# Attention with exact fp16 pairs and a gated MLP on one core: products with v seven tiles behind their scores in place of five, and copy, subtraction and transpose written one tile behind the exponential

## The chip, the cores and the metric

The kernel runs on one core of a Trainium2 chip. The metric is the device time of one execution in microseconds. Before the change three runs took 709.54 us in the median (708.9 to 712.29).

## The reference

Inputs are q, k, v of 4 batches, 8 heads, 768 rows, 64 columns, and the weights of a gated MLP. Attention is masked by a hash: a row's six sign bits of `q @ proj` must equal those of the key's row.

```python
mask = q_bucket[:, :, :, None] == k_bucket[:, :, None, :]
scores = scale * np.matmul(q, k.transpose(0, 1, 3, 2))
scores = np.where(mask, scores, -1000000000.0)
attn = softmax(scores)                      # maximum subtracted, exp, divided by the sum + 1e-9
x = attn @ v                                # then heads side by side: (4, 768, 512)
h = relu(x @ w_in); u, v = halves of h      # 512 and 512 columns
v_n = layer norm of v (no gain)
v_s = w_spatial @ v_n + b_spatial           # mixes the 768 rows
out = (u * v_s) @ w_out
```

## The kernel before

Each of the 32 heads is cut into six tiles of 128 query rows. A global count g = 6 * head + tile runs the main loop; iteration g writes the scores of tile g and the products with v of an older tile, and small pieces of everything else between. Values that need more than fp16 are kept as a pair of fp16 numbers, a rounded one and the rest.

A tile of the heads 0 and 8 to 31 goes through this chain:

- `scores` (L300, L301): four matmuls per tile on TensorE (PE), two per half of the keys, from the buffer `ab` of the head into a PSUM buffer `sp` (two of them). The hash mask is part of the second matmul.
- L302: VectorE (DVE) copies the scores to `ex` (four buffers) and takes the row maximum; L303 and L304: ScalarE (ACT) makes the bias `nb` and the exponential, in place.
- L307: ScalarE rounds `ex` to fp16 in `pp` (four buffers); L308: VectorE, or GpSimd (POOL) for one or two tiles of a head, subtracts to get the rest.
- L310: SyncE (SP) issues a transposing DMA from `pp` to `pt` (six buffers).
- `weighted` (L323 to L325): 18 matmuls with `pt` as weights and the split v (`vp`, two buffers, one per pair of heads) into the PSUM buffer `pv`. After a head's last tile, `normalize` divides by the sums and `transpose_x` brings a pair of heads, by another transposing DMA (`xt`), into the form that the MLP needs.

Heads 1 to 7 (KEYS) go another way without a transpose: their scores are made with keys on the partitions (`scores_k`, `weighted_k`), three tiles apart.

When all eight heads of a batch are done, its MLP is put in a queue of 28 units (`vps`, `ups`, `sps`, `ops`), and 28/48 of a unit is taken per iteration. The units of the last batch run after the last attention tile. `build` makes the buffer `ab` for the head two further on (DMAs from `hl` and `sg`); `load_qk`, `load_v`, `hash_rows`, `split_qk` and `split_v` work ahead by one to three pairs of heads.

The order of the instructions on each engine is not that of the text. Every piece is written with a place number, `at(g, k)` = 1000 * (g + 40) + k, and a scheduler issues per engine what has the lowest number and is ready by its own reckoning. `tc.issue_after(x)` keeps what is written inside it from being issued ahead of x. SP issues all loads and transposes in one queue; each waits in line for the one ahead. `st["tr"]` is the transpose written last.

The lines that set the distance are these:

```python
LAG = 5
...
while wv < N * NT and wv + (LAGK if wv // NT in KEYS else LAG) <= g:
```

Of the kernel before, what the change touches and what calls it, by code (L numbers as in the profile page):

```python
# [36 lines left out]
def lsh_attention_spatial_gating(  # L37
# [14 lines left out]
    NT = S // P  # L52
# [47 lines left out]
    st = {}  # L100
# [46 lines left out]
    def load_qk(p):  # L147
        b, r = divmod(p, NPAIR)
        qk = st["qk", p] = ld.tile([P, 2, S], F32, tag="qk", bufs=QKB, name=f"qk{p}")
        LQ.dma_start(out=qk, in_=kq[b, r])  # L150

    def load_v(p):
        b, r = divmod(p, NPAIR)
        if has_queries(p):
            v32 = st["v32", p] = ld.tile([P, 2 * NT, D], F32, tag="v32", bufs=1, name=f"v32_{p}")
            LQ.dma_start(out=v32, in_=v[b, r])

    def load_vf(p):
        b, r = divmod(p, NPAIR)
        if has_keys(p):  # L160
            LQ.dma_start(out=vf[p % 2][:, :, 0:D], in_=v[b, r])
# [4 lines left out]
    def has_queries(p):  # L166
        return not (2 * p in KEYS and 2 * p + 1 in KEYS)

    def hash_rows(p):
        qk = st["qk", p]  # L170
        hp = ps_m.tile([P, 512], F32, tag=MT, name=f"hp{p}")
        for j in range(4):
            nc.tensor.matmul(
                hp[32 * j:32 * j + 32, :HS], lhsT=pj,
                rhs=qk[:, 1 - j // 2, (j % 2) * HS:(j % 2 + 1) * HS],
                start=True, stop=True, tile_position=(0, 32 * j))
        s0 = wk.tile([P, HS], F16, tag="sg0", name=f"sg0_{p}")
        nc.vector.tensor_scalar(s0, hp[:, :HS], 0.0, hv[:, 0:1], op0=ALU.is_gt, op1=ALU.subtract)
        s1 = wk.tile([P, HS], F16, tag="sg1", bufs=2, name=f"sg1_{p}")
        nc.vector.tensor_scalar(s1, s0, hv[:, 1:2], None, op0=ALU.mult)  # L180
        st["sg", p] = s1

    def split_qk(p):
        qk = st["qk", p]
        hl = wk.tile([P, 4, S], F16, tag="hl", bufs=1, name=f"hl{p}")
        nc.scalar.activation(hl[:, 1:3], qk, AF.Copy, scale=SQ)
        nc.vector.scalar_tensor_tensor(out=hl[:, 0], in0=qk[:, 1], scalar=SQ, in1=hl[:, 2], op0=ALU.mult, op1=ALU.subtract)
        nc.vector.scalar_tensor_tensor(out=hl[:, 3], in0=qk[:, 0], scalar=SQ, in1=hl[:, 1], op0=ALU.mult, op1=ALU.subtract)
        st["hl", p] = hl
# [29 lines left out]
    def split_v(p):  # L219
        if not has_queries(p):  # L220
            return
        v32, t = st["v32", p], vp[p % 2]
        nc.scalar.activation(t[:, :, D:2 * D], v32, AF.Copy, scale=SQ)
        nc.vector.scalar_tensor_tensor(out=t[:, :, 0:D], in0=v32, scalar=SQ, in1=t[:, :, D:2 * D], op0=ALU.mult, op1=ALU.subtract)
# [38 lines left out]
    def scores_k(n, i):  # L263
        t = ab[n % NAB]
        ps = ps_sc.tile([P, 2, 512], F32, tag="sc", name=f"sp{n}_{i}")[:, :, :HS]
        ks = slice(i * P, (i + 1) * P)
        for c in range(2):
            cs = slice(c * HS, (c + 1) * HS)
            nc.tensor.matmul(ps[:, c], lhsT=t[:, 1, ks], rhs=t[:, 0, cs], start=True, stop=False)  # L269
            nc.tensor.matmul(ps[:, c], lhsT=t[:, 2, ks], rhs=t[:, 3, cs], start=False, stop=True)  # L270
        ex = wk.tile([P, S], F32, tag="pt", bufs=PTB, name=f"ex{n}_{i}")
        st["ex", n, i] = nc.scalar.activation(ex.rearrange("p (c q) -> p c q", c=2), ps, AF.Exp, scale=ISQ).ins
        st["pt", n, i] = ex
# [11 lines left out]
    def scores(n, i):  # L285
        if n in KEYS:
            scores_k(n, i)
            return
        t = ab[n % NAB]
        if i == 0:  # L290
            st["nb", n] = wk.tile([P, NT], F32, tag="nb", bufs=3, name=f"nb{n}")
            st["mx", n] = wk.tile([P, NT], F32, tag="mx", bufs=4, name=f"mx{n}")
        mx, nb = st["mx", n][:, i:i + 1], st["nb", n][:, i:i + 1]
        ex = wk.tile([P, 2, HS], F32, tag="ex", bufs=EB, name=f"ex{n}_{i}")
        qs = slice(i * P, (i + 1) * P)
        ps = ps_sc.tile([P, 2, 512], F32, tag="sc", name=f"sp{n}_{i}")[:, :, :HS]
        K = P if n % 2 and n >= NH else P - 1
        for c in range(2):
            cs = slice(c * HS, (c + 1) * HS)
            nc.tensor.matmul(ps[:, c], lhsT=t[:, 0, qs], rhs=t[:, 1, cs], start=True, stop=False)  # L300
            nc.tensor.matmul(ps[:, c], lhsT=t[0:K, 3, qs], rhs=t[0:K, 2, cs], start=False, stop=True)  # L301
        nc.vector.tensor_scalar(ex, ps, -float(2 ** 28), None, op0=ALU.max, op1=ALU.max, accum_out=mx)  # L302
        nc.scalar.activation(nb, mx, AF.Copy, scale=-ISQ)  # L303
        st["ex", n, i] = nc.scalar.activation(ex, ex, AF.Exp, bias=nb, scale=ISQ).ins  # L304
        at(NT * n + i + G_H, 50)
        pp = wk.tile([P, 2, 2, HS], F16, tag="pp", bufs=PB, name=f"pp{n}_{i}")
        nc.scalar.copy(pp[:, 0], ex)  # L307
        (nc.gpsimd if i in (PL_POOL if n >= 2 * NH else PL_POOL1) else nc.vector).tensor_tensor(out=pp[:, 1], in0=ex, in1=pp[:, 0], op=ALU.subtract)  # L308
        pt = st["pt", n, i] = wk.tile([P, 2 * NT, P], F16, tag="pt", bufs=PTB, name=f"pt{n}_{i}")
        st["tr"] = nc.sync.dma_start_transpose(out=pt, in_=pp.rearrange("p g c k -> p (g c k)")).ins  # L310
# [147 lines left out]
    N = B * NH  # L458
    NP = B * NPAIR

    PL_POOL = (2,)
    KEYS = {1, 2, 3, 4, 5, 6, 7}
# [14 lines left out]
    EB = 4  # L477
    PTB = 6
    XTB = 6
    LAG = 5  # L480
    XL_ENG = nc.vector
    G_S = 0
    G_H = 1
# [12 lines left out]
    def at(g, k):  # L496
        tc.cur_priority = int(1000 * (g + 40) + k)
# [16 lines left out]
    rml = [(NT * n + i - NT - LEAD, n, i) for n in sorted(KEYS) for i in range(NT)]  # L514
    for g in range(N * NT + LAG):
        n, i = divmod(g, NT)
        if n < N:
            at(g + G_S, 0)
            scores(n, i)
            r = n // 2  # L520
            at(g + G_P, 300)
            if g == 0:
                hash_rows(1)
                split_qk(1)
                split_v(0)
                load_qk(2)
                load_v(1)
                load_vf(0)
                load_vf(1)
            at(g + G_M, 100)  # L530
            while rml and rml[0][0] <= g:
                row_max(*rml.pop(0)[1:])
            at(g + G_P, 300)
            stack = ExitStack()
            if n not in KEYS:
                stack.enter_context(tc.issue_after(st["tr"]))
            if BQ_S[n + 2 >= NH] is nc.scalar or BQ_H[n + 2 >= NH] is nc.scalar:
                stack.enter_context(tc.issue_after(st["ex", n, i]))
            if i == BI and n + 2 < N:
                build(n + 2)  # L540
            if n % 2 == 0:
                if i == 4 and 0 < r < NP - 1:
                    load_vf(r + 1)
                if i == 5 and r + 1 < NP:
                    split_v(r + 1)
                    mean_v(r + 1)
                if i == 4 and r == 0:
                    mean_v(0)
            else:
                if i == 2 and r + 2 < NP:  # L550
                    hash_rows(r + 2)
                if i == 3 and r + 2 < NP:
                    split_qk(r + 2)
                if i == 5 and r + 3 < NP:
                    load_qk(r + 3)
                if i == 1 and r + 2 < NP:
                    load_v(r + 2)
            stack.close()
        while wv < N * NT and wv + (LAGK if wv // NT in KEYS else LAG) <= g:
            m, j = divmod(wv, NT)  # L560
            wv += 1
            at(g + G_V, 200)
            weighted(m, j)
            if j == NT - 1:
                at(g + G_N, 250)
                normalize(m)
                if m % 2:
                    transpose_x(m // 2)
                    if m % NH == NH - 1:
                        queue += mlp_units(m // NH)  # L570
        at(g + G_W, 500)
        while wdone < W_AT(g):
            wdone += 1
            next(wg, None)
        if queue and n < N:
            credit += 28.0 / DEN
            at(g + G_U, 400)
            while queue and credit >= 1.0:
                queue.pop(0)()
                credit -= 1.0  # L580
# [44 lines left out]
```

## Time and profile before

| | |
|---|---|
| median of three runs | 709.54 us |
| profiled execution | 708.95 us |
| its span, first to last instruction | 707.2 us |
| mean granted TensorE clock | 0.964 |
| instructions | 14858 |
| DMA packets, bytes | 286555, 111.51 MB |

The profile's page gives each engine's busy time and share of the span; the waits say for which instruction's end an engine stood idle, with the total, the number of times and the longest. "A <- B" reads "A waited for B". L numbers are lines of the kernel, tile names are those of the program without their numbers, and SPq is the queue of DMA issues on SP. PEld is TensorE's loading of weights, which runs beside its matmuls.

### The profile page before, as it was taken

How to read it: one execution, taken by the hardware profiler on the slowest of the kernel's cores; microseconds unless marked ns; L12 is line 12 of the kernel's file. 1: busy time of each engine (PE TensorE's matmuls, PEld its weight loads, DVE VectorE, ACT ScalarE, POOL GpSimd, SP SyncE). 2: the span in 40 equal slices, each digit the busy share in tenths (PEclk: the TensorE clock that was granted, in tenths of full speed). 3: DMA queues.
4: the chain of work that ended last, by engine and by line, in shares of the span. 5: the costliest groups of instructions: out<-in, count | busy, mean ns of one | idle time of the engine just before them, and what ended most of it. 6: DMA issues, size and time to landing. Idle time of an engine off the chain costs nothing.

```text
span 707.2 us, 14858 instructions
## 1 busy us (share of the span) xinstructions
PE 618.5 (87%) x5735; PEld 391.0 (55%) x5735; DVE 511.3 (72%) x961; ACT 454.2 (64%) x806; POOL 222.0 (31%) x215
## 2 busy tenths in 40 slices
PE   1668798999796989999796999899888999999997
PEld 0236676778453655565454565565445655655553
DVE  4665698388888897779699897899697987725100
ACT  1444477567686868777588786868677688724121
POOL 5111434454324452152002162033022530322513
PEclk9999798699899999999998999999999999999999
DMA  9557557353698979998989999999989899950011
GB/s 242 143 109 185 125 154 161 89 163 106 134 185 176 184 161 199 217 194 192 206 153 214 165 197 191 201 185 215 214 171 151 158 180 206 156 132 1 0 45 45
DMA packets 286555, 111.51 MB, mean 158 GB/s; under 512 B 270356, under 2 KB 273428, under 8 KB 286484
## 3 DMA queue, kind: packets, MB, share of 16 engines
q1 hardware_dynamic: 284180, 109.67, 77.0%
q10 hardware_dynamic: 2304, 0.89, 0.6%
q8 instruction: 45, 0.74, 0.4%
q14 instruction: 26, 0.21, 0.1%
HBM read 28.33 MB, written 6.29 MB: 49 GB/s over the span
## 4 chain that ended last, share of the span: by engine, by line
PE 48%; DMA 22%; DVE 11%; issue 7%; SPq 4%; ACT 4%; POOL 4%; ACTq 0%; DVEq 0%; POOLq 0%
DMA pt<-pp 14%; PE sps L428 7%; PE ops L443 7%; PE vps L372 6%; PE ups L413 6%; PE pv L282 4%; DMA ab<-hl 4%; PE sp L300 3%; PE sp L301 3%; PE pv L323 3%; SPq L310 2%; PE pv L325 2%; PE pv L324 2%; DVE ex L302 2%; PE sp L269 1%
## 5 line engine op out<-in xcount | busy, mean ns | idle before, releaser
L302 DVE TENSOR_SCALAR_CACHE_REDUCE ex<-sp 128x768 f32<-128x768 f32 x150 | 141.8, 951 | 42.1 <-PE sp L301 39.7
L304 ACT ACTIVATE ex<-ex,nb 128x768 f32<-128x768 f32 x150 | 139.3, 932 | 7.4 <-ACT nb L303 4.5
L323 PE MATMUL pv<-vp,pt 128*128 128x65 f16 x900 | 105.7, 196 | 43.3 <-DMA pt<-pp 42.7
L307 ACT CAST pp<-ex 128x768 f16<-128x768 f32 x150 | 123.7, 826 | 10.5 <-DMA pt<-pp 5.2
L308 DVE TENSOR_TENSOR pp<-ex,pp 128x768 f16<-128x768 f32 x116 | 123.1, 1064 | 9.5 <-ACT pp L307 8.9
L308 POOL TENSOR_TENSOR pp<-ex,pp 128x768 f16<-128x768 f32 x34 | 57.9, 1702 | 218.0 <-ACT pp L307 175.3
L323 PEld LDWEIGHTS <-pt 128*128 128x128 f16 x900 | 85.5, 100 | 70.7 <-DMA pt<-pp 61.8
L300 PE MATMUL sp<-ab 128*128 128x384 f16 x300 | 102.1, 340 | 14.4 <-DMA ab<-hl 9.3
L324 PE MATMUL pv<-vp,pt 128*128 128x64 f16 x900 | 105.4, 196 | 0.0
L325 PE MATMUL pv<-vp,pt 128*128 128x65 f16 x900 | 104.8, 197 | 0.0
L301 PE MATMUL sp<-ab 127*128 127x384 f16 (+1 forms) x300 | 102.2, 341 | 0.6 <-DMA ab<-sg 0.6
L428 PE MATMUL sps<-ws,vn 128*128 128x384 f16 x576 | 100.7, 326 | 0.5 <-DVE sy L432 0.5
L324 PEld LDWEIGHTS <-pt 128*128 128x128 f16 x900 | 85.9, 99 | 10.7 <-issue 1.9
L325 PEld LDWEIGHTS <-pt 128*128 128x128 f16 x900 | 86.0, 99 | 2.3 <-issue 0.6
L428 PEld LDWEIGHTS <-vn 128*128 128x128 f16 x576 | 54.3, 98 | 35.1 <-issue 1.8
L282 PEld LDWEIGHTS pv<-vf,ex 128*128 128x128 f32 x504 | 69.2, 210 | 3.2 <-issue 1.0
L372 PE MATMUL vps<-wi,xt 128*128 128x512 f16 x288 | 67.4, 382 | 3.2 <-DMA xt<-xs 3.2
L413 PE MATMUL ups<-xt,wi 128*128 128x384 f16 x384 | 69.4, 333 | 0.0
L443 PE MATMUL ops<-wo,g 128*128 128x512 f16 x288 | 67.8, 379 | 1.0 <-ACT o L447 0.9
L282 PE MATMUL pv<-vf,ex 128*128 128x65 f32 x504 | 68.0, 289 | 0.0
L303 ACT ACTIVATE nb<-mx 128x1 f32<-128x1 f32 x150 | 29.3, 197 | 57.2 <-DVE ex L302 56.2
L433 POOL TENSOR_TENSOR sy<-sy,u 128x384 f32<-128x384 f32 x32 | 35.9, 1125 | 75.5 <-DVE sy L432 54.5
(91 smaller groups left out, 920.8 us busy)
## 6 DMA issues: line engine op xcount, KB each, us to landing
qk<-kq SPq DMA_DIRECT2D x16, 768.0 KB
ab<-hl SPq DMA_DIRECT2D x34, 192.0 KB
out<-o SPq DMA_DIRECT2D x24, 256.0 KB
v<-v SPq DMA_DIRECT2D x13, 384.0 KB
raw<-w_in SPq DMA_DIRECT2D x16, 256.0 KB
ab<-hl SPq DMA_DIRECT2D x7, 384.0 KB
pt<-pp SPq DMA_TRANSPOSE x150
raw<-w_sp SPq DMA_DIRECT2D x12, 192.0 KB
```

Source lines behind the costliest of these rows:

```text
L282: nc.tensor.matmul(acc[:, qi, :], lhsT=ex[:, qi * P:(qi + 1) * P], rhs=vf[p % 2][:, 2 * i + e, :], start=(i == 0 and qi == 0), stop=(i == ...
L300: nc.tensor.matmul(ps[:, c], lhsT=t[:, 0, qs], rhs=t[:, 1, cs], start=True, stop=False)
L301: nc.tensor.matmul(ps[:, c], lhsT=t[0:K, 3, qs], rhs=t[0:K, 2, cs], start=False, stop=True)
L302: nc.vector.tensor_scalar(ex, ps, -float(2 ** 28), None, op0=ALU.max, op1=ALU.max, accum_out=mx)
L304: st["ex", n, i] = nc.scalar.activation(ex, ex, AF.Exp, bias=nb, scale=ISQ).ins
L307: nc.scalar.copy(pp[:, 0], ex)
L308: (nc.gpsimd if i in (PL_POOL if n >= 2 * NH else PL_POOL1) else nc.vector).tensor_tensor(out=pp[:, 1], in0=ex, in1=pp[:, 0], op=ALU.subtract)
L323: nc.tensor.matmul(acc, lhsT=pt[:, c, :], rhs=vh, start=(i == 0 and c == 0), stop=False)
L324: nc.tensor.matmul(acc[:, 0:D], lhsT=pt[:, c, :], rhs=vl, start=False, stop=False)
L325: nc.tensor.matmul(acc, lhsT=pt[:, NT + c, :], rhs=vh, start=False, stop=(i == NT - 1 and c == NT - 1))
L428: nc.tensor.matmul(ps[:, :HS], lhsT=vn[gv][:, c, d * P:(d + 1) * P], rhs=ws[gw][:, c, hs], start=(k == 0), stop=(k == 3 * NT - 1))
L443: nc.tensor.matmul(ps, lhsT=gt[h][gg][:, c, j * P:(j + 1) * P], rhs=wo[gw][:, c, :], start=(k == 0), stop=(k == 3 * NF - 1))
```

## The change

`LAG` becomes 7, so the products of tile t are written in iteration t + 7. The second half of `scores` (copy, subtraction, transpose) becomes a function `halves`, called one iteration later, after the loads and builds of that iteration; its place number is the same as before, (t + 1, 50), since it was put one tile behind already. What is written under `issue_after(st["tr"])` now refers to the transpose of tile g - 2, and not of tile g. `split_v` and `load_v` are tied to `LAG`: the split for the next pair moves from tile 5 of the even head to tile 1 of the odd one, two tiles later, and the load behind it from tile 1 to tile 2.

```diff
         st["ex", n, i] = nc.scalar.activation(ex, ex, AF.Exp, bias=nb, scale=ISQ).ins
-        at(NT * n + i + G_H, 50)
+        st["e32", n, i] = ex
+
+    def halves(n, i):
+        ex = st.pop(("e32", n, i))
         pp = wk.tile([P, 2, 2, HS], F16, tag="pp", bufs=PB, name=f"pp{n}_{i}")
...
-    LAG = 5
+    LAG = 7
+    SPL = 1
...
-            if n not in KEYS:
+            if n not in KEYS and 'tr' in st:
                 stack.enter_context(tc.issue_after(st["tr"]))
...
                 if i == 5 and r + 1 < NP:
-                    split_v(r + 1)
                     mean_v(r + 1)
...
-                if i == 1 and r + 2 < NP:
+                if i == LAG - NT and r + 1 < NP:
+                    split_v(r + 1)
+                if i == LAG - NT + 1 and r + 2 < NP:
                     load_v(r + 2)
             stack.close()
+        if 0 <= g - SPL < N * NT and (g - SPL) // NT not in KEYS:
+            at(g - SPL + G_H, 50)
+            halves(*divmod(g - SPL, NT))
```

The built order shows what the scheduler makes of it. In names such as `pt22_1_5695` the first numbers are head and tile, the last one a running number. On PE, in the middle of head 22, the first products of tile 22_1 stood behind the scores of tile 23_0:

```order
L300 MATMUL sp23_0_5912<-ab3_85 128x384
L301 LDWEIGHTS ab3_85
L301 MATMUL sp23_0_5912<-ab3_85 128x384
L323 LDWEIGHTS pt22_1_5695
L323 MATMUL pv22_5864<-vp1_95,pt22_1_5695 128x65
```

Now, with new line numbers (L326 is the former L323):

```order
L300 MATMUL sp23_2_5942<-ab3_85 128x384
L301 LDWEIGHTS ab3_85
L301 MATMUL sp23_2_5942<-ab3_85 128x384
L326 LDWEIGHTS pt22_1_5672
L326 MATMUL pv22_5896<-vp1_95,pt22_1_5672 128x65
```

The products moved behind two more score tiles. Over all tiles, 93 of 150 stood five score tiles behind and 22 six; now 75 stand seven and 47 six behind.

On SP, in the same place of the program, the order of loads and transposes was this (`xt10` is the transpose of x, `ab` a head's buffer, `v32` and `qk` loads from memory):

```order
L355 DMA_TRANSPOSE xt10_5846<-xs10_5575 128x12x128
L310 DMA_TRANSPOSE pt22_5_5860<-pp22_5_5857 128x12x128
L310 DMA_TRANSPOSE pt23_0_5923<-pp23_0_5920 128x12x128
L217 DMA ab1_83<-hl12_5500 64x1536
L310 DMA_TRANSPOSE pt23_1_5962<-pp23_1_5959 128x12x128
L156 DMA v32_13_5964<-v 128x768
L310 DMA_TRANSPOSE pt23_2_6020<-pp23_2_6017 128x12x128
L310 DMA_TRANSPOSE pt23_3_6061<-pp23_3_6058 128x12x128
L310 DMA_TRANSPOSE pt23_4_6121<-pp23_4_6118 128x12x128
L310 DMA_TRANSPOSE pt23_5_6185<-pp23_5_6182 128x12x128
L150 DMA qk14_6187<-kq 128x1536
```

and is now:

```order
L313 DMA_TRANSPOSE pt22_5_5851<-pp22_5_5848 128x12x128
L313 DMA_TRANSPOSE pt23_0_5894<-pp23_0_5891 128x12x128
L217 DMA ab1_83<-hl12_5438 64x1536
L358 DMA_TRANSPOSE xt10_5878<-xs10_5609 128x12x128
L313 DMA_TRANSPOSE pt23_1_5964<-pp23_1_5961 128x12x128
L156 DMA v32_13_5959<-v 128x768
L313 DMA_TRANSPOSE pt23_2_6000<-pp23_2_5997 128x12x128
L313 DMA_TRANSPOSE pt23_3_6056<-pp23_3_6053 128x12x128
L150 DMA qk14_6085<-kq 128x1536
```

The transpose of x moved two places back and the load of q and k two places forward; `ab` and `v32` kept theirs.

On PE at the end of attention, the last products (tile 31_5) stood between two pieces of the units `ops2_4` and `ops2_3`. The end of the piece ahead of them:

```order
L443 MATMUL ops2_4_8585<-wo1_107,g2_0_1_8167 128x512
L443 LDWEIGHTS g2_1_1_8168
L443 MATMUL ops2_4_8585<-wo0_106,g2_1_1_8168 128x512
L323 LDWEIGHTS pt31_5_8447
L323 MATMUL pv31_8449<-vp1_95,pt31_5_8447 128x65
```

Now the products of 31_4 stand right ahead of them, and all of `ops2_3` to `ops2_5` with the unit `sps2_3_1` behind them:

```order
L327 MATMUL pv31_8425<-vp1_95,pt31_4_8350 128x64
L328 LDWEIGHTS pt31_4_8350
L328 MATMUL pv31_8425<-vp1_95,pt31_4_8350 128x65
L326 LDWEIGHTS pt31_5_8397
L326 MATMUL pv31_8425<-vp1_95,pt31_5_8397 128x65
```

Eighteen matmuls of `ops` moved from ahead of the last products to behind them, and the unit `sps2_3_1` with them, while `sps2_1_1` and two product tiles came behind the last scores.

## The prediction

> **What bounds the kernel now.** I read the page's first lines, then TensorE's own waits by stage, then one wait followed back by hand, then the load of each engine in the stage where the waits lie.
>
> ```profile
> span 707.2 us, 14858 instructions
> PE 618.5 (87%) x5735; PEld 391.0 (55%) x5735; DVE 511.3 (72%) x961; ACT 454.2 (64%) x806; POOL 222.0 (31%) x215
> ```
>
> TensorE (PE) is idle for 707.2 - 618.5 = 88.7 us and no other engine is near it in the mean. The next view sums each stage: 180 to 632 us is the stage of the 144 query tiles with transposes (heads 8 to 31), after it only the last batch's gating stage is left. Columns: stretch, length, busy time of PE, PEld, DVE, ACT, POOL, granted clock, DMA share, GB/s.
>
> ```profile
> 180.00:632.00 452.00, 407.12 (x4379) 249.85 (x4378) 373.70 (x692) 338.57 (x593) 133.72 (x100) 0.97 0.98 183
> 632.00:707.00 75.00, 70.42 (x384) 37.26 (x382) 13.71 (x34) 19.20 (x39) 22.00 (x22) 1.00 0.09 29
> 0.00:180.00 180.00, 140.98 (x975) 103.89 (x976) 123.87 (x237) 96.44 (x176) 66.29 (x93) 0.92 0.58 147
> ```
>
> The middle stage spends 452 / 144 = 3.14 us a tile, and TensorE idles 452 - 407.1 = 44.9 us of it. The last 75 us are TensorE alone, and the change does not alter them. TensorE's waits in the middle stage, the three that are over 1 us:
>
> ```profile
> PE pv L323 <- DMA pt<-pp: 36.6, 32, 3.2
> PE sp L300 <- DVE ex L302: 3.8, 7, 0.9
> PE vps L372 <- DMA xt<-xs: 3.2, 1, 3.2
> ```
>
> So 36.6 of 44.9 us is one thing: the products wait for the transposed exponentials, 32 times, never over 3.2 us. Is that a chain that is too long for the distance between scores and products, or a chain that cannot go faster? Here is tile 1 of head 22, from the timeline (start, duration, engine, line).
>
> ```profile
> 441.28 0.32 PE L300 MATMUL sp<-ab 128*128 128x384 f16 x1
> 442.49 0.33 PE L300 MATMUL sp<-ab 128*128 128x384 f16 x1
> 443.52 0.95 DVE L302 TENSOR_SCALAR_CACHE_REDUCE ex<-sp 128x768 f32<-128x768 f32 x1
> 445.42 0.86 SPq L150 DMA_DIRECT2D qk<-kq  x1
> 445.94 0.93 ACT L304 ACTIVATE ex<-ex,nb 128x768 f32<-128x768 f32 x1 [0.65 <-ACT nb L303]
> 446.76 2.35 SPq L310 DMA_TRANSPOSE pt<-pp  x1
> 447.24 0.82 ACT L307 CAST pp<-ex 128x768 f16<-128x768 f32 x1
> 448.40 0.95 DVE L308 TENSOR_TENSOR pp<-ex,pp 128x768 f16<-128x768 f32 x1
> 449.17 0.91 SPq L217 DMA_DIRECT2D ab<-hl  x1
> 450.17 7.13 SPq L310 DMA_TRANSPOSE pt<-pp  x3
> 452.70 0.20 PE L323 MATMUL pv<-vp,pt 128*128 128x65 f16 x1
> 453.26 0.32 PE L300 MATMUL sp<-ab 128*128 128x384 f16 x1
> 455.78 0.20 PE L323 MATMUL pv<-vp,pt 128*128 128x65 f16 x1 [1.71 <-DMA pt<-pp]
> ```
>
> The scores start at 441.28. Maximum, exponential, copy and subtraction end at 449.35; most of those 8.1 us is queueing, the four operations themselves take 0.95 + 0.93 + 0.82 + 0.95 = 3.65. The transpose is issued at 450.17, behind a transpose (446.76) and a load (449.17) that themselves stood behind a 768 KB load (445.42). The products start at 455.78, 14.5 us after the scores. Meanwhile TensorE had done the five next score tiles (the last, head 23 tile 0, at 453.26) and had nothing else in its order. Five tiles at 3.14 us are 15.7 us: the chain and the distance are equally long, and any burst (a load, a normalization) makes TensorE wait.
>
> **The change, part by part.** *Nothing is added or removed.* Each tile still issues one exponential, copy, subtraction and transpose.
>
> *Seven tiles in place of five.* In the built order the products of that tile stand behind head 23 tile 2: two score tiles further, 2 x 3.14 = 6.3 us more room. Every one of the 32 waits is at most 3.2 us, so each alone would be covered. Two kinds I leave standing. First the ramp into head 8, where there is no lead yet; then the stretches in which VectorE is full, because there TensorE would only wait one step earlier, at the scores. TensorE's waits on pt at 185 to 192, 215 to 226 and 370 to 391 us, and VectorE's load (third busy column) in the latter two:
>
> ```profile
> PE pv L323 <- DMA pt<-pp: 3.1, 2, 2.0
> PE pv L323 <- DMA pt<-pp: 4.6, 3, 2.5
> PE pv L323 <- DMA pt<-pp: 6.0, 4, 2.8
> ...
> 215.00:220.00 5.00, 2.97 (x29) 1.41 (x27) 4.96 (x12) 1.96 (x5) 1.14 (x1) 1.00 0.56 107
> 220.00:225.00 5.00, 2.19 (x26) 1.25 (x26) 5.00 (x9) 5.00 (x11) 2.53 (x2) 1.00 1.09 267
> 370.00:375.00 5.00, 3.73 (x50) 2.20 (x49) 4.96 (x14) 3.34 (x9) 1.64 (x1) 1.00 1.14 235
> 380.00:385.00 5.00, 4.73 (x60) 3.69 (x61) 5.00 (x10) 4.44 (x8) 0.00 (x0) 0.50 1.15 226
> ```
>
> Term 1: -(36.6 - 3.1 - 4.6 - 6.0) = **-22.9 us**. Its bounds: 0, if the chain is at its own limit; -33.5, if all but the ramp goes.
>
> *What is late next.* With 22 us less, VectorE's 373.7 us fill 87% of the stage in place of 83%, and TensorE meets its two score buffers more often. That row is 3.8 us now (sp <- DVE ex); I take it twice: **+3.8**, bounds 0 and +10.6 (the waits left standing above, a second time).
>
> *Copy, subtraction and transpose one tile behind.* The number that places them is (tile + 1, 50) before and after, so only the written order moves. In the built order 134 of 150 copies stood ahead of the next tile's exponential, now 131; on VectorE some subtractions fall behind one more maximum (0.95 us) and some come one forward. Room 6.3 us covers that: 0, bounds -0.95 and +0.95.
>
> *Loads on SP.* What waits for "the last transpose" now waits for one two tiles older, so SP takes the head builds and the q/k loads one to three places earlier, and the transposes of x two tiles later. Around head 23 the order has ab, xt, v and qk with only three pt transposes between them, where xt stood two tiles ahead and qk four behind v. Landing times from the chain of waits:
>
> ```profile
> 1.19 4.39 DMA qk<-kq
> 391.83 4.13 DMA v<-v
> 495.86 4.76 DMA xt<-xs
> ```
>
> A bunch of three can hold up a transpose by some 4 us at most, within the 6.3; **+2**, bounds 0 and 12 pairs x 1.66 (one transpose issue, row below) = +20.
>
> *Six transposed buffers, seven tiles.* The transpose of tile t must now wait until the products of t - 6 are done, and these stand behind the scores of t + 1, no longer ahead of those of t. On SP, in order, everything behind it waits along. In the tile above, the scores of t + 1 start at 442.49; the products of one tile take 0.6 us (452.70 to 453.26), so the buffer would come free near 443.9 (two times 0.7, scores and products, after 442.49), while the subtraction ended at 449.35: 5.4 us to spare. 0, bounds 0 and the rival below.
>
> *v.* The split of v comes two tiles later and its load one tile behind it; the first products that read it are later by two tiles as well, twelve tiles behind the split in both orders, and the products that read what it overwrites still end one tile ahead of it. 0.
>
> *The end.* In the order of before, 18 matmuls of `ops` separate the last products from the tile ahead of them; now the last five product tiles stand in a row and the fillers behind them.
>
> ```profile
> 613.95 0.32 PE L300 MATMUL sp<-ab 128*128 128x384 f16 x1
> 623.18 4.05 PE L443 MATMUL ops<-wo,g 128*128 128x512 f16 x18
> 627.07 0.19 PE L323 MATMUL pv<-vp,pt 128*128 128x65 f16 x1
> L310 SPq DMA_TRANSPOSE pt<-pp x150: 1307/1657/3611, 28.4 to 621.3; - x150
> ```
>
> Last scores to last products are 13.1 us, with 3.9 us of them `ops`; now two product tiles more stand between them and no `ops`, so TensorE arrives 3.9 - 2 x 0.6 = 2.7 us earlier. The last transpose, issued at 621.3, lands at 626.9 if it takes the 5.6 us of tile 22_1, and TensorE would be there at 624.4: at most +2.5. The queues are emptier here, so **+1**, bounds 0 and +2.5; behind it 54 matmuls of fillers cover the last transpose of x.
>
> *The start.* Head 0 is the only tile row there. The waits on pt of 25 to 180 us:
>
> ```profile
> PE pv L323 <- DMA pt<-pp: 6.1, 4, 2.2
> ```
>
> They may go, or the key heads behind head 0 may come up to two tiles later: 0, bounds -6.1 and +6.3.
>
> Sum: -22.9 + 3.8 + 2 + 1 = -16.1, span 691.1. The profiled execution took 708.95 us for a span of 707.2, so 692.8; the median of the runs is 0.6 above that execution: **693.5 us**.
>
> **The clock.** After such waits the granted clock falls: 0.50 in 380 to 385 above, and less sharply around the others.
>
> ```profile
> 215.00:230.00 15.00, 9.54 (x87) 5.22 (x86) 12.98 (x28) 10.42 (x21) 6.88 (x5) 0.89 0.95 190
> 340.00:352.00 12.00, 7.32 (x92) 4.59 (x93) 7.32 (x13) 6.62 (x12) 0.00 (x0) 0.86 1.07 196
> 370.00:395.00 25.00, 17.83 (x196) 11.42 (x195) 21.16 (x47) 20.55 (x37) 6.79 (x5) 0.80 1.18 215
> ```
>
> The missing clock is 0.11 x 15 + 0.14 x 12 + 0.20 x 25 = 8.3 us. Two of the three stretches are those I leave standing, so I take none of it. [...]
>
> **Rivals.**
> *A, TensorE becomes the only bound.* All 33.5 us go and the 8.3 us of clock with them: -33.5 - 8.3 + 3.8 + 1 = -37 us, **672 us**. For it: no wait is longer than 3.2 us. Against: DMA share 0.98 and VectorE full for stretches.
>
> *B, the chain is at its own limit.* The DMA share of the stage is 0.98 and the transposes fill it; a longer distance only stores tiles, and TensorE waits as long in other places. Term 1 is 0, the new waits are 0 too, and the end's +1 stays: **710 us**. Against: while TensorE waits the DMA share is as low as 0.56 (215 to 220), and VectorE idles 78 us of the stage.
>
> *C, slower: SP held by the sixth buffer.* If a transpose has to wait for the products of t - 6, all later loads and transposes wait with it, and the waits move rather than go. It decides once TensorE reaches the products of t - 6 over 5.4 us later than I reckon, say with two 18-matmul units between them. SP's own waits:
>
> ```profile
> SPq L310 <- PE pv L325: 54.9, 40, 3.2
> ```
>
> That row names TensorE's products already, though by the order this buffer is free long before; if it is real and comes in place of the 36.6, the time is 709.5 + 54.9 - 36.6 = **728 us**. [...]
>
> **How the numbers follow.** Forecast 0.52 (685 to 703), A 0.14, B 0.20, C 0.14. A change under 0.5% (3.5 us) cannot be told from none. Faster: 0.52 + 0.14 + 0.02 of B's edge = 0.68; same: most of B, 0.17; slower: C and a little of B, 0.15. The range leaves out the far part of A and most of C: 680 to 712.
>
> **What would show it.** Right: the row pv <- pt of the stage falls from 36.6 to about 14 us, sp <- DVE ex rises to about 8, the stage shortens by some 16 us with TensorE's busy time unchanged, VectorE's share rises to 0.86. B: pv <- pt is smaller but sp <- DVE ex has taken its place. C: transposes start within 1 us after the products of six tiles before, and SP's queue stands still there. I am wrong if the order costs more than I see: late xt for `vps`, or products that wait at the end.

## The result, and the profile after

The changed kernel takes 690.56 us in the median of four runs (689.38 to 695.97), the one before 709.56 (708.9 to 712.29). The ratio is 0.974, with a 95% interval of 0.9683 to 0.9797. The forecast was 693.5 us, so the total was right. What follows shows that the sum behind it was right only in part: the larger share of the gain comes from the half of the change that the prediction priced at next to nothing (0 for the instructions that move, +2 for the loads that this releases).

The profiled execution took 690.15 us. The head of its page:

```profile
span 688.3 us, 14846 instructions
PE 606.2 (88%) x5735; PEld 385.5 (56%) x5735; DVE 517.4 (75%) x961; ACT 451.0 (66%) x806; POOL 229.0 (33%) x215
```

TensorE is idle for 688.3 - 606.2 = 82.1 us, only 6.6 less than before; the other 12.3 us went out of its busy time, although it runs the same 5735 matmuls. The missing clock (one minus the granted clock, times the length; 0.964 was granted before, 0.972 after) fell by 707.2 x 0.036 - 688.3 x 0.028 = 6.2 us. That it accounts for half of the 12.3 is an estimate, which takes a us of missing clock as one of busy time; for the rest the rows name no cause. A forecast by waits alone cannot have seen any of it.

To see where, both executions are cut at the same four events: the first scores of head 8 (175.9 us before, 164.3 after), the last scores, the last products, the end. Columns as in the prediction: stretch, length, busy PE, PEld, DVE, ACT, POOL, granted clock, DMA share, GB/s. The kernel before:

```profile
0.00:175.90 175.90, 136.88 (x942) 100.31 (x943) 119.90 (x228) 95.29 (x174) 65.39 (x93) 0.92 0.58 147
175.90:613.90 438.00, 393.16 (x4225) 242.49 (x4224) 368.80 (x684) 332.20 (x581) 128.57 (x95) 0.97 0.98 185
613.90:627.70 13.80, 13.80 (x174) 9.09 (x171) 7.40 (x13) 5.93 (x11) 6.05 (x7) 1.00 0.76 117
627.70:707.20 79.50, 74.69 (x405) 39.12 (x401) 15.18 (x38) 20.80 (x42) 22.00 (x22) 1.00 0.11 35
```

and the changed one:

```profile
0.00:164.30 164.30, 127.17 (x944) 94.11 (x945) 118.03 (x215) 92.08 (x166) 64.95 (x90) 0.95 0.61 155
164.30:590.20 425.90, 386.49 (x4171) 240.28 (x4170) 376.55 (x696) 331.88 (x587) 133.99 (x97) 0.98 1.02 191
590.20:601.90 11.70, 11.24 (x192) 8.46 (x188) 6.98 (x13) 5.62 (x10) 5.97 (x6) 1.00 0.95 163
601.90:688.30 86.40, 81.26 (x439) 42.67 (x436) 15.89 (x39) 21.41 (x43) 24.05 (x25) 1.00 0.10 33
```

The differences are -11.6, -12.1, -2.1 and +6.9, together -18.9 us. Two of the four rows were put at zero in the prediction: the first stage, which gives the same as the middle one, and the tail, which got longer. TensorE's busy time in the middle stage falls by 6.7 us and rises by 6.6 in the tail: matmuls of the MLP have moved to the end.

TensorE's waits in the middle stage of the changed kernel (164 to 590 us; total, times, longest); those of before are the three rows in the prediction:

```profile
PE pv L326 <- DMA pt<-pp: 18.3, 19, 2.1
PE sp L300 <- DVE ex L302: 11.3, 14, 2.3
PE vps L375 <- DMA xt<-xs: 5.6, 3, 4.1
PE sps L431 <- DVE sg L178: 2.2, 2, 1.3
PE ups L416 <- DVE sg L178: 1.1, 1, 1.1
```

The waits for the transposes are halved (36.6 to 18.3), and 13.2 us of other waits stand in their place: VectorE at the scores 3.8 to 11.3, the transposed x 3.2 to 5.6, and `sg`, 3.3 us that were not in the list (the signs of a hash, read from a buffer in the pool that the MLP's matmuls use too).

### The profile page after: what moved, and what is told of

Its sections match the earlier page's. It is cut to its first block, busy times and chain, and to the rows that moved or that the text cites. A ratio compares the mean times of both kernels' runs of the same rounds, so it can differ in the third digit from the quotient of the medians.

```text
span 688.3 us, 14846 instructions
## 1 busy us (share of the span) xinstructions
PE 606.2 (88%) x5735; PEld 385.5 (56%) x5735; DVE 517.4 (75%) x961; ACT 451.0 (66%) x806; POOL 229.0 (33%) x215
## 3 DMA queue, kind: packets, MB, share of 16 engines
q1 hardware_dynamic: 284180, 109.67, 79.1%
## 4 chain that ended last, share of the span: by engine, by line
PE 50%; DMA 19%; DVE 14%; issue 7%; ACT 5%; POOL 2%; SPq 2%; ACTq 1%; DVEq 0%; POOLq 0%
DMA pt<-pp 11%; PE sps L431 10%; PE ops L446 8%; PE vps L375 6%; PE ups L416 6%; PE sp L300 4%; PE sp L301 4%; PE pv L326 2%; PE pv L282 2%; PE pv L328 2%; DVE ex L302 2%; DMA ab<-hl 2%; PE pv L327 2%; DMA xt<-xs 2%; DVE pp L311 2%
## 5 line engine op out<-in xcount | busy, mean ns | idle before, releaser
L302 DVE TENSOR_SCALAR_CACHE_REDUCE ex<-sp 128x768 f32<-128x768 f32 x150 | 141.4, 949 | 18.3 <-PE sp L301 17.3
L311 DVE TENSOR_TENSOR pp<-ex,pp 128x768 f16<-128x768 f32 x116 | 120.4, 1039 | 24.3 <-ACT pp L310 23.4
L311 POOL TENSOR_TENSOR pp<-ex,pp 128x768 f16<-128x768 f32 x34 | 61.3, 1803 | 219.3 <-ACT pp L310 180.4
L310 ACT CAST pp<-ex 128x768 f16<-128x768 f32 x150 | 123.1, 825 | 12.3 <-DMA pt<-pp 8.6
L326 PE MATMUL pv<-vp,pt 128*128 128x65 f16 x900 | 103.5, 195 | 23.8 <-DMA pt<-pp 23.5
L300 PE MATMUL sp<-ab 128*128 128x384 f16 x300 | 101.1, 337 | 24.1 <-DVE ex L302 14.1
L326 PEld LDWEIGHTS <-pt 128*128 128x128 f16 x900 | 85.0, 99 | 42.9 <-DMA pt<-pp 32.6
L328 PE MATMUL pv<-vp,pt 128*128 128x65 f16 x900 | 103.8, 196 | 0.0
L327 PE MATMUL pv<-vp,pt 128*128 128x64 f16 x900 | 103.5, 194 | 0.0
L327 PEld LDWEIGHTS <-pt 128*128 128x128 f16 x900 | 84.9, 98 | 11.0 <-issue 1.1
L328 PEld LDWEIGHTS <-pt 128*128 128x128 f16 x900 | 84.9, 98 | 3.3 <-issue 0.3
L282 PEld LDWEIGHTS pv<-vf,ex 128*128 128x128 f32 x504 | 64.6, 198 | 3.1 <-issue 0.5
L282 PE MATMUL pv<-vf,ex 128*128 128x65 f32 x504 | 63.9, 277 | 0.0
L404 POOL TENSOR_TENSOR vn<-vr,vn 128x512 f16<-128x512 f32 x24 | 31.8, 1349 | 78.8 <-ACT vn L403 78.8
```

Of the source, the lines that this page charges most:

```text
L282: nc.tensor.matmul(acc[:, qi, :], lhsT=ex[:, qi * P:(qi + 1) * P], rhs=vf[p % 2][:, 2 * i + e, :], start=(i == 0 and qi == 0), stop=(i == ...
L326: nc.tensor.matmul(acc, lhsT=pt[:, c, :], rhs=vh, start=(i == 0 and c == 0), stop=False)
L327: nc.tensor.matmul(acc[:, 0:D], lhsT=pt[:, c, :], rhs=vl, start=False, stop=False)
L328: nc.tensor.matmul(acc, lhsT=pt[:, NT + c, :], rhs=vh, start=False, stop=(i == NT - 1 and c == NT - 1))
```

## The experiments

The granted clock differs between executions of one kernel (0.960 to 0.972 in the four timed runs of the change), so both kernels were profiled a second time, to see whether the time at half clock ahead of head 8 belongs to the order or to the single execution. Half clock means stretches in which the granted clock was 0.50. The kernel before again:

> The kernel before, unchanged, for a second trace. If the time at half clock ahead of head 8 belongs to the order: 24 to 30 us of it again and head 8's first scores at 175 to 177 us. [...]

The changed kernel again:

> The changed kernel, unchanged, for a second trace. Belonging to the order: 10 to 14 us at half clock ahead of head 8 and its first scores at 163 to 166 us; a matter of one execution: up to 27 us, and 172 us.

They took 708.73 and 691.68 us. Head 8 began at 172.3 and at 166.4 us, in neither trace where the first one of its kernel would put it (175 to 177, 163 to 166): part of the first stage is a matter of the single execution. All traces of this study, cut at the same events (us; the first column of numbers is the median of the timed runs, or the one execution):

| kernel | time | to head 8's first scores | to the last scores | to the last products | to the end |
|---|---|---|---|---|---|
| before | 709.56 | 175.9 | 438.0 | 13.8 | 79.4 |
| before, second trace | 708.73 | 172.3 | 441.4 | 13.8 | 79.4 |
| after | 690.56 | 164.3 | 425.9 | 11.7 | 86.4 |
| after, second trace | 691.68 | 166.4 | 425.4 | 11.6 | 86.4 |
| distance 7 alone | 709.44 | 172.7 | 435.1 | 13.2 | 86.4 |
| second half alone | 695.0 | 167.0 | 432.9 | 13.8 | 79.4 |
| second half alone, head 0 only | 700.51 | 165.8 | 438.4 | 13.8 | 79.4 |
| second half alone, heads 8 to 31 only | 701.67 | 174.1 | 432.6 | 14.0 | 79.4 |
| the older transpose alone | 694.3 | 168.8 | 429.5 | 14.0 | 79.4 |
| change, distance 7 from head 8 on only | 694.65 | 165.3 | 430.0 | 11.7 | 86.4 |
| change, distance 7 for head 0 only | 693.26 | 163.0 | 435.3 | 13.8 | 79.4 |
| before, no hold in the first iteration | 706.41 | 169.0 | 440.9 | 13.8 | 79.4 |
| before, mean of v two tiles later | 714.87 | 181.3 | 441.0 | 13.9 | 79.4 |
| change, MLP units at 28/45 | 693.38 | 166.0 | 433.2 | 11.1 | 80.3 |

The same kernel repeats to 3.6 us in the first two stages, in opposite directions, and to 0.1 in the last two. With the means of the two traces each, the change gives -8.8, -14.1, -2.2 and +7.0, together some -18 us. The experiments have one trace each, so their first two stages are known to some 4 us and no better.

**Distance 7 alone.** The theory of the prediction gives it most of the gain.

```diff
-    LAG = 5
+    LAG = 7
...
-                if i == 5 and r + 1 < NP:
-                    split_v(r + 1)
...
-                if i == 1 and r + 2 < NP:
+                if i == 1 and r + 1 < NP:
+                    split_v(r + 1)
+                if i == 2 and r + 2 < NP:
                     load_v(r + 2)
```

> The kernel before with the distance of seven tiles alone (the split and load of v moved along); copy, subtraction and transpose stay written in the scores. Theory 1 (the longer distance is the gain): 688 to 695 us. Theory 3 (the gain comes from loads and builds being released by a transpose two tiles older): 703 to 711 us.

It took 709.44 us against 708.51, ratio 1.0018 (0.999 to 1.0046). Its waits in the middle stage and the stage's row:

```profile
PE pv L323 <- DMA pt<-pp: 22.5, 20, 2.9
PE sp L300 <- DVE ex L302: 12.6, 15, 2.7
...
173.00:608.00 435.00, 393.96 (x4172) 244.42 (x4170) 377.52 (x692) 331.78 (x584) 132.44 (x95) 0.96 0.99 185
```

The products wait 14.1 us less and the scores 8.8 us more: with more tiles in hand TensorE waits for VectorE at its two score buffers (12.6 us in place of 3.8). The stage shrinks by 4.6 us (435.1 against a mean of 439.7), the tail grows by 7.0, and nothing is left. TensorE's busy time in the stage does not fall either (393.96 us after 393.16), though 53 matmuls fewer stand there: the clock was 0.96 in this trace. With both halves the same work took 386.49 us at 0.98. Averaged over the 132 tiles of heads 9 to 30, products start 17.4 us after their scores before, and 21.2 us with distance 7; the copy ends 7.5 and 8.4 us after the scores, and VectorE's reading of the scores 3.2 and 3.8. The chain gets 3.8 us more room and uses 0.8 of it up itself, most of that (0.6) by queueing in front of VectorE.

**The second half alone.** Copy, subtraction and transpose as in the change, distance 5.

```diff
-    LAG = 7
+    LAG = 5
     SPL = 1
...
                 if i == 5 and r + 1 < NP:
+                    split_v(r + 1)
                     mean_v(r + 1)
...
-                if i == LAG - NT and r + 1 < NP:
-                    split_v(r + 1)
-                if i == LAG - NT + 1 and r + 2 < NP:
+                if i == 1 and r + 2 < NP:
                     load_v(r + 2)
```

> The other half alone: copy, subtraction and transpose written one iteration later, distance five, v as before. Theory 1: no change, 706 to 712 us. Theory 3: 692 to 700 us.

It took 695.0 us, ratio 0.9828 (0.9775 to 0.9882): 13.5 of the 19 us. The part that the prediction priced at zero is the larger one, taken alone. The two stages of its trace:

```profile
49.20:167.00 117.80, 107.80 (x823) 86.10 (x821) 85.13 (x175) 73.62 (x140) 45.86 (x63) 0.92 0.54 143
167.00:600.00 433.00, 388.27 (x4224) 240.53 (x4223) 382.08 (x695) 335.07 (x590) 136.98 (x99) 0.98 1.00 188
```

Half of the gain lies ahead of head 8 (167.0 against a mean of 174.1), half in the middle stage (432.9 against 439.7), and the tail is as before. In the middle stage it is not idle time that goes: TensorE is idle for 433.00 - 388.27 = 44.7 us, as before (438.00 - 393.16 = 44.8). Its busy time is 4.9 us less for the same matmuls, and the missing clock 6.8 us in place of 11.9 and 13.7 in the two traces of before.

**The distance in one stage, with the second half kept.** Where does distance 7 add to it?

```diff
-        while wv < N * NT and wv + (LAGK if wv // NT in KEYS else LAG) <= g:
+        while wv < N * NT and wv + (LAGK if wv // NT in KEYS else LAG if wv >= NT else 5) <= g:
```

> The changed kernel with distance five for head 0 and seven from head 8 on. Theory 1 (the gain lies in heads 8 to 31, in the products' waits): 688 to 694 us. Theory 2 (over half of it, 11.6 of 18.9 us, lies ahead of head 8, where a wait for POOL at 119 us and 17.1 us at half clock behind it are gone): head 8's first scores stay near 176 us and the time is 699 to 704 us.

```diff
-        while wv < N * NT and wv + (LAGK if wv // NT in KEYS else LAG) <= g:
+        while wv < N * NT and wv + (LAGK if wv // NT in KEYS else 5 if wv >= NT else LAG) <= g:
```

(and v as in the kernel before)

> The changed kernel with distance seven for head 0 alone and five from head 8 on. Theory 1: 706 to 711 us. Theory 2: head 8's first scores near 164 us and a time of 696 to 700 us.

They took 694.65 (ratio 0.983, 0.9775 to 0.9886) and 693.26 us (0.9803, 0.9748 to 0.9859). Neither agrees with a theory as it was put: the first had head 8 begin at 165.3 us and not near 176, the second was faster than either range. In the table, the three traces with distance 7 from head 8 on have middle stages of 425.4 to 430.0 us, the two with distance 5 and the second half everywhere 432.9 and 435.3: some 7 us, and 2 more up to the last products, against 7 in the tail. So behind the second half the distance is worth about -2 us by these traces; one kernel with distance 5, the older transpose alone (below), has 429.5 too. By time, distance 7 from head 8 on is no faster than the second half alone (694.65 and 695.0). The whole change (ratio 0.974, 0.9683 to 0.9797) is 2.7 us below distance 7 for head 0 only and 4.4 below the second half alone, and the intervals overlap: that the distance adds something is likely and not settled.

**The second half in one stage.** The rival was that it acts only in one of the two stages, ahead of head 8 or behind.

```diff
+        if n == 0:
+            at(NT * n + i + G_H, 50)
+            halves(n, i)
...
-        if 0 <= g - SPL < N * NT and (g - SPL) // NT not in KEYS:
+        if 0 <= g - SPL < N * NT and (g - SPL) // NT not in KEYS and g - SPL >= NT:
```

> The second half alone (distance five), and only from head 8 on; head 0 keeps copy, subtraction and transpose in its scores, and its loads wait for its own transposes. Theory 2 (the gain lies ahead of head 8): head 8's first scores stay near 173 to 176 us, time 703 to 710 us. Theory 3 (the gain is the release of loads and builds by an older transpose in heads 8 to 31): 694 to 699 us.

The same with `n > 0` and `g - SPL < NT`, so that it is in head 0 only:

> The complement: the second half alone, and only for head 0; from head 8 on as before. Theory 2: head 8's first scores near 165 us, time 695 to 700 us. Theory 3: 705 to 711 us.

They took 701.67 (0.9875, 0.9836 to 0.9915) and 700.51 us (0.987, 0.982 to 0.992), between the ranges of the two theories, each of which had one stage alone. Each acts in its own stage: from head 8 on it shortens the middle stage (432.6 against 439.7) and leaves the first as it was (174.1); in head 0 it shortens the first (165.8) and hardly the middle (438.4). Against 709.75 us they gain 8.1 and 9.2 us, more together than the 13.5 of both at once; intervals of some 3 us either way allow for that.

**What of the second half does it: the written order, or the older transpose?** The second half also makes everything under `issue_after` refer to an older transpose. Here the kernel before keeps its distance and its written order, and only that reference is changed; the loads of weights refer to one transpose older, as in the change.

```diff
+        st["tr2"], st["tr1"] = st.get("tr1"), st.get("tr")
...
-            if n not in KEYS:
-                stack.enter_context(tc.issue_after(st["tr"]))
+            if n not in KEYS and st["tr2"] is not None:
+                stack.enter_context(tc.issue_after(st["tr2"]))
...
-            with tc.issue_after(st["tr"]):
+            with tc.issue_after(st["tr1"]):
```

> The kernel before with distance five and its written order; only what is held until a transpose is issued is held until one two iterations older (the weights' loads one iteration older), as in the change, in head 0 and from head 8 on. If this release is all that the second half does: the 695 us of the run with the second half alone, 692 to 698 us. If the written order (which tile takes which buffer at the step from head 0 to head 1) has a part of its own: 699 to 704 us. If the release does nothing: 706 to 711 us.

It took 694.3 us against 707.03, ratio 0.9815 (0.975 to 0.9879): all that the second half gives. Its middle stage, and TensorE's waits there:

```profile
168.80:598.00 429.20, 388.92 (x4216) 240.68 (x4215) 371.89 (x683) 330.31 (x581) 130.82 (x95) 0.98 1.00 189
PE pv L323 <- DMA pt<-pp: 28.9, 33, 2.3
PE sp L300 <- DVE ex L302: 4.5, 7, 1.5
```

The waits for the transposes fall by some 8 us without a longer distance, and unlike there the scores do not wait more. Builds, hashes, splits and loads no longer have to be issued behind the transpose of the tile just written. It is not that a tile's chain got shorter: between the copy's end and the transpose's issue a tile took 3.7 us before and 3.4 here, but the copy ends 0.5 us later, so that from scores to issue it is 11.2 and 11.4 us.

The clock rises with the release. The seven executions of the kernel before that were timed beside these four had a granted clock of 0.954 in the mean, these 0.971: 32.6 us of missing clock and 20.1. With the second half alone it was 0.969 beside 0.955, with the distance alone 0.955 beside 0.955. Missing clock is reckoned over busy and idle time alike: in the middle stage, by the row above, its busy time is 4.2 us below that of before and its idle time 4.6. So that the release is worth 12.7 us is shown; how much of it is shorter waits, how much is clock, whether the clock follows from the waits, and which of the released works matters, is not.

**The hold in the first iteration.** In the change there is no transpose yet when iteration 0 is written, so nothing is held there. Is that the gain at the start?

```diff
-            if n not in KEYS:
+            if n not in KEYS and g > 0:
```

> The kernel before, with one thing of the change: in iteration 0 the builds and loads are not held until the first transpose is issued. Theory 2a (what helps ahead of head 8 is that the first builds stand ahead of the first transpose on SP): key heads start by 49 us, head 8 by 167 us, time 696 to 701 us. Theory 2b (it is the order of head 0's later loads, or the wait for POOL and the half clock behind it by chance of the order): 703 to 711 us.

It took 706.41 us, ratio 0.9958 (0.9916 to 1.0). The first exponential of the key heads comes at 49.2 us and not at 51.7 and 51.3, as in the changed kernel (49.1 and 49.3); that is the 2.3 us by which this part is shorter. The first stage of this one trace is 169.0 us against a mean of 174.1; the rest of that lies in the key heads. With 3.3 us by time and an interval that reaches 1.0 the hold is a part of the start's gain at most: the second half in head 0 alone gave 9.2.

**The wait in the key heads.** In both traces of before, TensorE waits for GpSimd near 119 us, and its clock is low behind it (0.51 and 0.50 in 120 to 130 us of the first trace, 0.75 and 0.56 in the second). The wait and the clock before, first trace:

```profile
PE mp L237 <- POOL vc L235: 2.2, 1, 2.2
...
115.00:120.00 5.00, 3.22 (x23) 2.25 (x22) 3.42 (x8) 1.94 (x4) 3.02 (x6) 1.00 1.30 225
120.00:125.00 5.00, 4.03 (x17) 3.46 (x18) 2.90 (x4) 4.97 (x12) 2.69 (x5) 0.51 0.38 97
125.00:130.00 5.00, 5.00 (x23) 3.96 (x23) 1.98 (x3) 2.20 (x4) 2.07 (x3) 0.50 0.44 123
130.00:135.00 5.00, 5.00 (x21) 3.80 (x20) 1.39 (x4) 2.46 (x5) 1.33 (x3) 0.50 0.23 73
135.00:140.00 5.00, 5.00 (x34) 4.31 (x33) 2.48 (x4) 2.76 (x5) 3.19 (x5) 0.79 0.28 79
```

TensorE stands 1.8 us of a 5 us slice, and then runs at half clock for 17.1 us, busy for nearly all of them (16.13 of the 17.0 us from 120.1 to 137.1). The wait does not occur in the changed kernel. To take it away alone, the mean of v for the next pair was written two tiles later:

```diff
                 if i == 5 and r + 1 < NP:
-                    mean_v(r + 1)
...
             else:
+                if i == 1 and r + 1 < NP:
+                    mean_v(r + 1)
```

> The kernel before, with the sum over v of the next pair of key heads written two tiles later, so that its matmul on TensorE stands further behind the load and POOL's additions. Theory 2 with the half clock as its cause: the wait for POOL at 119 us goes, and the 17.1 us at half clock behind it; head 8's first scores at 167 to 169 us, time 699 to 702 us. If the wait is not the cause: 706 to 712 us.

A miss: 714.87 us, ratio 1.0083 (1.0044 to 1.0122). The wait on GpSimd is gone, the stage's waits by that view come to the same (12.5 us against 12.7), and the whole stage of the key heads (first exponential of the key heads to head 8) ran at 0.86 of the clock:

```profile
51.50:181.30 129.80, 117.37 (x798) 92.54 (x798) 91.91 (x190) 77.54 (x153) 51.03 (x68) 0.86 0.48 131
```

So this wait is not needed for the low clock. Nor does the low clock of this one trace explain the loss: over the ten runs the mean clock was that of the kernel before (0.955 and 0.954). What does stays open.

**The tail.** Two iterations fewer lie between the end of a batch and the end of the attention, and each takes 28/48 of an MLP unit. More per iteration gives the units back:

```diff
-    DEN = 48
+    DEN = 45
```

(in the changed kernel)

> The changed kernel with the MLP's units taken a little faster, 28/45 per iteration in place of 28/48, so that the third batch's units are used up by the last attention tile as they were at distance five. If distance seven loses 5 us at the end because two iterations fewer are left for these units, and the middle stage has idle TensorE time for them: from the last products to the end some 79 us in place of 86, time 684 to 687 us. If the middle stage grows by as much: 689 to 692 us.

It took 693.38 us (ratio to before 0.981, 0.9764 to 0.9856), 1.4 us above the range for a middle stage that grows by as much. The tail is 80.3 us again, and the middle stage took it all back, with 36.3 us of waits on the two rows in place of 29.6:

```profile
166.00:599.20 433.20, 390.34 (x4207) 244.09 (x4206) 377.00 (x698) 335.02 (x591) 138.86 (x100) 0.98 1.02 189
PE pv L326 <- DMA pt<-pp: 21.7, 23, 2.9
PE sp L300 <- DVE ex L302: 14.6, 18, 2.3
```

So the tail's 7 us is not won back by this number; no other was run. Part of what looks like a gain in the middle stage is MLP work moved to the end. None of the versions run is faster than the changed kernel.

## Why the prediction was right, and where it was not

*What bounds it.* Right: the waits on the transposed exponentials were the largest piece of the middle stage, and the change halved them.

*Term 1, -22.9 us for the distance.* Of the right mechanism, mis-sized, and not the distance's alone. The row fell by 18.3 us with both halves together; the distance alone takes 14.1, the older transpose alone some 8. And what left the row did not all leave the stage: its idle time fell from 44.8 to 39.4 us, its busy time, expected unchanged, by 6.7.

*What is late next, +3.8.* Right in kind, mis-sized: the scores' wait rose by 7.5 us, within the bound of 10.6 that was named. The condition had been seen (VectorE at 87% by the sum; by the row after 376.55 / 425.9 = 88%), and doubling the row was too little.

*Loads on SP, +2.* The wait for xt rose by 2.4 us, about what was named; the 3.3 us on `sg` were not in the sum. But the release that this step prices as a small loss is, in the experiment, a gain: wrong in sign.

*Copy, subtraction and transpose one tile behind, 0.* This step failed, and it is the one that matters. It looked at where the three instructions go, for which 0 was fair, and not at what is held by the transpose they end in. The held work was named in the next step, as a burden for SP. The runs show that release to be worth 12.7 us by itself (694.3 against 707.03).

*The start, 0.* Failed: the first stage is 8.8 us shorter by the means. Of this 2.3 us lie ahead of the key heads; the rest is in them, and most of that is clock by the estimate below, as far as two traces each can tell that differ by 3.6 and 2.1 us among themselves.

*The end, +1, and "the last 75 us ... the change does not alter them".* Failed: the last products come 2.2 us sooner after the last scores, as worked out (2.7), but the tail is 7.0 us longer. The step counted the matmuls around the last products and not the units of MLP that two fewer iterations leave over; a rate per iteration (28/48) was in the text.

*Six buffers, 0, and rival C.* Right. The smallest time between the end of the products of t - 6 and the issue of the transpose of t was 6.1 us before and is 1.6 after, and for no tile came the buffer later than the subtraction (with distance 7 alone it did for two, by 0.2 and 0.4 us). SP's row that was to carry C still stands in the changed kernel, at 46.0 in place of 54.9 us:

```profile
SPq L313 <- PE pv L328: 46.0, 37, 2.9
```

It is not a wait for a buffer: no tile waited for one, though the margin has shrunk to 1.6 us before the issue and to 0.3 before the end of the subtraction.

*Rival A.* Not so: 39 us of idle time are left in the stage. *Rival B* gave 710 us; distance 7 alone took 709.44, and partly for B's reason (8.8 of 14.1 us turned into another wait), with the tail for the rest. It is the second half that kept the whole from being B.

*The clock.* None was taken. In these traces the missing clock of the middle stage hardly moved (11.9 us before and 13.7 in its second trace, 10.2 and 11.9 after), so taking none of the 8.3 us there fits them. The low end of the forecast's range, 685 us, is the sum less these 8.3, the author's estimate; no run shows that they go with the waits: in the first traces the waits for the transposes halved (36.6 to 18.3), and the missing clock of the stage fell by 1.7 us. By the timed runs the clock as a whole did rise: the kernel before had 0.954 to 0.956 in the mean of each group of runs, the four runs of the changed kernel 0.967, and the two traces of before, with 0.964 and 0.958, lie above their kernel's mean. So this row is not settled. In the key heads, which had not been looked at, the clock moved in the traces too. Before, first and second trace:

```profile
51.70:175.90 124.20, 112.16 (x817) 89.67 (x818) 89.27 (x186) 76.78 (x150) 50.14 (x67) 0.89 0.54 140
```

```profile
51.30:172.30 121.00, 108.99 (x817) 87.45 (x818) 89.92 (x186) 76.61 (x149) 49.18 (x67) 0.92 0.56 144
```

and after, in the same order:

```profile
49.10:164.30 115.20, 105.32 (x822) 84.25 (x820) 87.13 (x172) 73.89 (x141) 48.78 (x64) 0.95 0.56 146
```

```profile
49.30:166.40 117.10, 108.14 (x821) 86.61 (x820) 86.78 (x172) 74.04 (x141) 48.62 (x64) 0.92 0.55 143
```

TensorE was at half clock for 27.3 and 20.5 us before and for 10.5 and 18.8 after. Half of that, the missing clock, is 11.9 in the mean before and 7.3 after; taken as time lost, an estimate, it is 4.6 us of gain. The same matmuls did take longer there: in the first trace of before those of L269 took 524 ns in the mean at 125 to 137 us (clock 0.50) and 326 ns at 145 to 160 us (1.00), those of L282 406 and 271 ns.

So the total was right because errors cancelled: term 1 came with more new waits than reckoned and 7 us of tail, and gains that were not in the sum, the release and a higher clock, which the runs do not separate, made up for it. That the sum came within 3 us was luck.

## What to carry to other kernels

When a step is moved in a program whose order is set by "not ahead of x", list what hangs on x before pricing the step: here letting go of it two tiles earlier was worth 12.7 us, and the moved instructions by themselves nothing that could be seen. A longer distance between producer and consumer here moved a wait to the next full buffer (8.8 of 14.1 us) and left two iterations' MLP work over for the end (7.0 us); count both before the waits that go. A time that comes out as forecast does not prove the terms; only the run of each half alone did.

## What the runs showed of the hardware that was not expected

The length of the key heads' stage, over the 14 traces of this study, is 107.6 to 111.7 us plus half of the time that TensorE spent at half clock in it, and that time goes from 10.2 us (the stage 115.3 us long) to 37.5 us (129.8 us). Two executions of one kernel differ by 7 to 8 us in it: the same wait of 2.2 us near 119 us was followed by 17.1 us at half clock in one trace of before and by 6.8 us in the other. The latter:

```profile
120.00:125.00 5.00, 3.01 (x14) 2.59 (x15) 3.00 (x4) 4.90 (x10) 2.79 (x7) 0.75 0.82 128
125.00:130.00 5.00, 5.00 (x25) 4.07 (x26) 1.98 (x3) 3.08 (x7) 2.43 (x4) 0.56 0.36 84
130.00:135.00 5.00, 5.00 (x40) 4.13 (x39) 2.80 (x6) 3.91 (x8) 2.73 (x4) 1.00 0.35 113
```

In the first trace the granted clock was 0.50 in all of 79.1 to 89.3 and 120.1 to 137.1 us, and 1.00 from 137.2 us to head 8. Work on TensorE did not end the low clock there at once: it was busy through 125 to 135 us at 0.50, with 23 and 21 matmuls in 5 us, where the second trace has 40 in 5 us at 1.00. What keeps it low there stays open; the idle stretches were not filled with other matmuls to see whether the low clock goes with them.
